# Two pairs' k and q loaded first, on two queues, and the steps of attention put in another order

## The chip, the cores and the metric

One core of a Trainium2 chip runs the kernel. Its engines work beside each other, each through its own queue in order: TensorE (PE) multiplies, VectorE (DVE) and ScalarE (ACT) work elementwise, GpSimd (POOL) as well, and SyncE (SP) issues most of the DMAs; ACT can issue DMAs too. The metric is the time of one execution in microseconds (us) on the device.

## What is computed

```python
# q, k, v: (4, 8, 576, 64), k drawn 8 times as large; M_prev, z_prev, beta: a memory per head
scores = np.where(causal, -1e9, scale * q @ k.T)
local = softmax(scores) @ v
q_p = phi(q)                                   # elu + 1
mem_out = (q_p @ M_prev) / (q_p . z_prev + 1e-6)
g = sigmoid(beta)
x = g * mem_out + (1 - g) * local              # then (2304, 512): tokens by heads and columns
x = mish(x @ moe_w_in) @ moe_w_out             # 512 -> 2048 -> 512
return silu(x @ moe2_w_in) @ moe2_w_out
```

## The kernel before

**Attention** goes by pairs of heads: 4 batches of 4 pairs, 16 pairs. For each pair four loads bring the transposed k (`ldkT`, 128 x 640, 320 KB), the transposed q (`ldqT`, 288 KB), q by rows (`ldnq`, 288 KB) and v (`ldnv`, 320 KB). With the `nq` of a batch's first pair come z (256 KB, one row spread over all partitions) and y (two loads of 64 KB in pieces of 64 numbers). The host lays the inputs out for this.

Per pair, TensorE makes the scores in five blocks of queries (`s40` and `s41` for two halves of the widest, `s3`, `s2`, `s1`, and the small `s0`), each for both heads, into a ring `s` of four PSUM buffers (line 581, `s0` line 620). VectorE masks a block and takes its row minimum in one instruction (`r...`, line 574) into a ring `sm` of four buffers in SBUF; ScalarE takes the exponentials (`e...`, line 601). TensorE transposes the probabilities (`X1` to `X3`, `W`, `RT`, line 482), VectorE and ScalarE copy these out, and TensorE multiplies with v (`Vhi`, `Vlo`, line 678). Beside that runs the memory part: relu of q on ScalarE (`phu`, line 503), a subtraction on GpSimd (`phn`, line 501), an exponential on ScalarE (`phe`, line 502), then products with z and y on GpSimd and a sum on VectorE (`phr`, line 509).

**The gates.** Beta goes through an exponential on ScalarE (`gate exp`, line 430), five small steps on VectorE (`sig`, lines 433 to 437) and five copies on ScalarE (`spread`, lines 442 to 448). Pair 0's `phg`, `n00` and `zg` wait for them.

**The two layers** follow from about 180 us on (lines 950 to 1075). They use products of pairs of blocks, and need TensorE nearly all of the time. The weights of the first quarter of the first layer are decoded on VectorE during attention (lines 779 to 807).

**What sets the order.** `Steps.plan` simulates the engines, each with durations given by hand, and at each moment lets an engine take the ready step with the smallest key: the latest time at which it may start, plus a shift from the table `SHIFT` (by step and by pair, found by search). The result is the order in which each engine's instructions are issued. A load in the plan takes SP 1.4 to 1.6 us and lands 2.2 us later. Three loads are treated apart: pair 0's `ldkT` and `ldqT` are issued in `consts` ahead of the plan and count as landed at 4.7, pair 0's `ldnq` at 4.9, beta at 5.2.

At the start ACT's queue issues pair 0's k; SP's queue pair 0's q, then beta, and then what the plan says: pair 0's q by rows with z and y, pair 1's q and k, pair 1's q by rows, pair 0's v and so on.

Of the kernel before, what the change touches and what calls it, by code (L numbers as in the profile page):

```python
# [336 lines left out]
class Attn:  # L337
    GATED = ("phg", "n00", "zg")
    RINGS = {"s": 4, "t": 4, "sm": 4}
# [60 lines left out]
    def consts(self):  # L400
# [20 lines left out]
        self.load(0, "kT", nc.scalar)  # L421
        self.load(0, "qT")
# [67 lines left out]
    def steps(self, p):  # L490
# [6 lines left out]
        for nm in ("kT", "qT", "nq", "nv"):  # L497
            f["ld" + nm] = None if p == 0 and nm in ("kT", "qT") else lambda nm=nm: self.load(p, nm)
# [192 lines left out]
    def register(self, m):  # L691
# [3 lines left out]
        m.add(("gate", "exp"), "A", 0.2, [], exp, 25.0, 5.2)  # L695
        m.add(("gate", "sig"), "D", 1.0, [("gate", "exp")], sig, 26.0)
        m.add(("gate", "spread"), "A", 1.0, [("gate", "sig")], spread, 28.0)
        for p in range(B * NP):
            f = self.steps(p)
            due = (p + 2) * self.T  # L700
            for n, (e, d, deps, lag) in self.pair.ops.items():
                deps = [(p, x) for x in deps] + ([("gate", "spread")] if p == 0 and n in self.GATED else [])
                if p > 1 and n in ("s40", "s41"):
                    deps += [(p - 2, x) for x in self.SC + ["s0"]]
                if p == 0 and n in ("ldkT", "ldqT"):
                    d, lag = 0.0, 4.7
                if p == 0 and n == "ldnq":
                    d, lag = 0.6, 4.3
                m.mode[p, n] = 2 if n in self.VA else 3 if n == "s0" else 1 if e == "P" else 0
                m.add((p, n), e, d, deps, f[n], due, max(0.0, (p - 2) * self.T), lag, self.pair.cols.get(n))  # L710
            for r, h, fs, ls in self.pair.uses:
                m.hold("A." + r, (p, h), [(p, x) for x in fs], [(p, x) for x in ls])
            for r, (_, _, fs, ls, _) in self.TILES.items():
                m.hold("A." + r, p, [(p, x) for x in fs], [(p, x) for x in ls], order=p)
# [197 lines left out]
class Moe:  # L912
# [324 lines left out]
    ('gate', 'exp'): -539.87, ('gate', 'sig'): 1632.4, ('gate', 'spread'): 1083.76, ('a', 'ldkT'): -342.43,  # L1237
# [217 lines left out]
```

## Time and profile before

| | us |
|---|---|
| median of 3 runs | 953.03 (952.82 to 953.31) |
| the profiled execution | 955.01 |
| its span, first to last instruction | 953.2 |
| busy: TensorE | 926.1 (97%) |
| busy: VectorE | 670.5 (70%) |
| busy: ScalarE | 504.8 (53%) |
| busy: GpSimd | 143.2 (15%) |

The shares are means over stages. In the chain of work that ended last TensorE has 85%, VectorE 8%, ScalarE 4% and DMA 1%. The page cuts the span into 40 slices: VectorE and ScalarE are nearly full in the first seven, GpSimd too, and from the ninth on TensorE is full and the others are not. Rows of a timeline give the start, the duration, the engine and line, output and inputs, shapes, the count and in brackets how long the engine had stood idle and what ended that.

### The profile page before, as it was taken

The page shows a single profiled execution, that of the slowest core. Times are in us where ns is not written, and L with a number is a line of the kernel's source. Part 1 is how long each engine was busy: PE and PEld are TensorE (multiplying, and loading weights), DVE is VectorE, ACT ScalarE, POOL GpSimd, SP SyncE. Part 2 cuts the span into 40 slices and gives each one's busy share as a digit, 9 for nine tenths or more (in the row PEclk, how much of TensorE's full clock was granted, in tenths as well). Part 3 has the DMA queues.
Part 4 walks back from the last instruction along what each step waited for, and adds up shares of the span by engine and source line. Part 5 has one row for each costly group of instructions (what it writes and reads, how often), then busy time and mean ns, then how long its engine had stood idle before and what let it go on. Part 6 is the DMA issues. An engine that isn't in the chain of part 4 may idle for free.

```text
span 953.2 us, 17388 instructions
## 1 busy us (share of the span) xinstructions
PE 926.1 (97%) x6656; PEld 817.2 (86%) x6656; DVE 670.5 (70%) x1536; ACT 504.8 (53%) x1188; POOL 143.2 (15%) x175
## 2 busy tenths in 40 slices
PE   5989999899999999999999999999999999999998
PEld 3666666599999999999999999898999898989986
DVE  4899999897386759654957899866656765754333
ACT  5999999777455333434433647554434442433330
POOL 5778987400000000000000000000000000000000
PEclk9999999899999999999999999999999999999999
DMA  6545452456447612760375535704550374024412
GB/s 220 146 154 157 146 170 62 147 232 250 171 135 240 216 45 73 258 194 1 96 254 189 231 119 194 293 23 139 204 182 3 109 257 157 1 89 149 156 56 99
DMA packets 57219, 143.47 MB, mean 151 GB/s; under 512 B 6960, under 2 KB 24368, under 8 KB 57136
## 3 DMA queue, kind: packets, MB, share of 16 engines
q1 hardware_dynamic: 56992, 142.04, 43.7%
q8 instruction: 52, 0.85, 0.4%
q10 hardware_dynamic: 144, 0.33, 0.1%
q14 instruction: 31, 0.25, 0.1%
HBM read 104.60 MB, written 37.75 MB: 149 GB/s over the span
## 4 chain that ended last, share of the span: by engine, by line
PE 85%; DVE 8%; ACT 4%; issue 2%; DMA 1%; SPq 0%; POOL 0%; DVEq 0%; ACTq 0%; POOLq 0%
PE acc L1054 42%; PE psX L986 7%; PE psX L987 7%; PE psX L988 7%; PE psY L986 4%; PE psY L987 4%; PE psY L988 4%; DVE sm L574 2%; PE ps_t L678 2%; PE psW L987 2%; PE psW L988 2%; PE psW L986 2%; PE ps_s L581 2%; ACT Ph L601 1%; PE ps_t L482 1%
## 5 line engine op out<-in xcount | busy, mean ns | idle before, releaser
L1054 PE MATMUL acc<-g,w 128*128 128x320 f32 (+1 forms) x1152 | 218.9, 337 | 0.0
L1054 PE MATMUL acc<-w,g 128*128 128x512 f32 x864 | 214.4, 394 | 0.0
L1054 PEld LDWEIGHTS acc<-g,w 128*128 128x128 f32 x1152 | 183.9, 188 | 13.1
L1054 PEld LDWEIGHTS acc<-w,g 128*128 128x128 f32 x864 | 157.8, 188 | 30.5
L1017 ACT COPY vt<-psX 128x256 f32<-128x256 f32 (+1 forms) x192 | 75.2, 398 | 161.5 <-PE psX L988 154.9
L1075 DVE TENSOR_TENSOR xT<-acc,xT 128x512 f32<-128x512 f32 (+1 forms) x126 | 77.1, 613 | 93.0 <-PE acc L1054 92.2
L1027 DVE TENSOR_TENSOR g<-vt,g 128x512 fp32r<-128x512 f32 (+1 forms) x128 | 94.2, 754 | 34.7 <-ACT g L1026 33.8
L1015 DVE TENSOR_TENSOR vt<-psY,vt 128x256 f32<-128x256 f32 (+1 forms) x128 | 57.9, 456 | 85.4 <-ACT vt L1017 44.8
L1026 ACT CAST g<-vt 128x512 fp32r<-128x512 f32 (+1 forms) x128 | 83.3, 672 | 32.4 <-PE acc L1054 31.1
L987 PE MATMUL psX<-x,w 128*128 128x320 f32 (+1 forms) x256 | 76.3, 298 | 1.4 <-DVE x L950 1.4
L986 PE MATMUL psX<-x,w 128*128 128x320 f32 (+1 forms) x256 | 76.3, 298 | 0.0
L988 PE MATMUL psX<-x,w 128*128 128x320 f32 (+1 forms) x256 | 76.1, 297 | 0.0
L581 PE MATMUL ps_s<-kT,qT 64*128 64x288 f32 (+3 forms) x320 | 66.9, 474 | 7.2 <-DMA kT<-in_kT_dram 4.8
L1023 ACT ACTIVATE vt<-vt 128x512 f32<-128x512 f32 (+1 forms) x64 | 43.9, 685 | 49.0 <-DVE vt L1015 48.9
L574 DVE CUSTOM_DVE_ANT_0 sm<-ps_s,mask 128x192 f32<-128x192 f32 (+3 forms) x128 | 56.8, 470 | 7.0 <-PE ps_s L581 3.9
L1021 ACT ACTIVATE vt<-vt 128x256 f32<-128x256 f32 (+1 forms) x64 | 28.5, 445 | 62.0 <-DVE vt L1015 62.0
L1015 DVE TENSOR_TENSOR vt<-psW,vt 128x256 f32<-128x256 f32 (+1 forms) x64 | 29.1, 455 | 37.0 <-PE psW L988 36.6
L1022 ACT ACTIVATE vt<-psX 128x256 f32<-128x256 f32 (+1 forms) x64 | 26.0, 407 | 51.1 <-PE psX L988 50.9
L987 PEld LDWEIGHTS psX<-x,w 128*128 128x128 f32 x256 | 48.8, 191 | 3.3 <-DVE x L950 1.6
L986 PEld LDWEIGHTS psX<-x,w 128*128 128x128 f32 x256 | 48.6, 190 | 2.1 <-issue 0.3
L988 PEld LDWEIGHTS psX<-x,w 128*128 128x128 f32 x256 | 48.8, 191 | 0.0
L601 ACT ACTIVATE Ph<-sm,m 128x448 f32<-128x448 f32 (+1 forms) x64 | 46.2, 725 | 3.0 <-DVE m L574 2.8
(125 smaller groups left out, 2040.3 us busy)
## 6 DMA issues: line engine op xcount, KB each, us to landing
stg<-in_moe_w_in_dram SPq DMA_DIRECT2D x32, 512.0 KB, 4.9
stg<-in_moe_w_out_dram SPq DMA_DIRECT2D x32, 512.0 KB, 3.7
x<-sp SPq DMA_DIRECT2D x18, 640.0 KB, 4.3
x<-sp SPq DMA_DIRECT2D x18, 512.0 KB, 4.2
sp<-x SPq DMA_DIRECT2D x12, 640.0 KB, 4.0
sp<-x SPq DMA_DIRECT2D x12, 512.0 KB, 3.5
nv<-in_v_dram SPq DMA_DIRECT2D x16, 320.0 KB, 3.0
x1T<-sp01T SPq DMA_DIRECT2D x8, 640.0 KB, 5.3
```

What stands on the lines that cost most here:

```text
L574: nc.vector.tensor_tensor_reduce(out, ps, mask, -0.125, init, ALU.add, ALU.min, acc)
L581: nc.tensor.matmul(ps, lhsT=s["qT"][R[j], qcols(i)], rhs=s["kT"][R[j], k0 + cols.start:k0 + cols.stop], start=True, stop=True)
L601: nc.scalar.activation(ptile(i)[:, o:o + w] if i else G("P0")[:, 2], s[f"sm{i}{j}"], AF.Exp, bias=s[f"m{i}"][:, j:j + 1], scale=-1.0, accu ...
L986: nc.tensor.matmul(o, lhsT=W(0, kc), rhs=X(0, kc), start=(n in (1, 2, 7) and kc == 0), stop=False, skip_group_check=True)
L987: nc.tensor.matmul(o, lhsT=W(0, kc), rhs=X(1, kc), start=False, stop=False, skip_group_check=True)
L988: nc.tensor.matmul(o, lhsT=W(1, kc), rhs=X(0, kc), start=False, stop=(kc == 1), skip_group_check=True)
L1015: nc.vector.tensor_tensor(o, self.bank[q, to], o, op=ALU.add)
L1017: f[f"s{n}"] = lambda n=n: nc.scalar.copy(val(*at[n]), self.bank[q, "X"])
L1026: f[f"h{c}"] = lambda c=c: nc.scalar.copy(hi(c), val(c))
L1027: f[f"l{c}"] = lambda c=c: nc.vector.tensor_tensor(self.gt(q, c)[:, 1, :2 * tb], val(c), hi(c).bitcast(F32), op=ALU.subtract)
L1054: nc.tensor.matmul(y, lhsT=a, rhs=b, start=(c == 0 and k == 0), stop=(c == 1 and k == 5))
L1075: nc.vector.tensor_tensor(part, acc, part, op=ALU.add)
```

## The change

In `consts`, both pairs 0 and 1 have their transposed k loaded from ACT's queue and their transposed q from SP's; pair 0's q by rows with z and y comes next, and beta last. The planner is told when these land (`FIRST`), takes beta's exponential as possible from 8.5 on instead of 5.2, and issues no other load before 4.2. The table `SHIFT` has other values for the steps of attention, the splits of the first layer's first block and the first group of weights; for the rest of the two layers it is the same. (`SHIFT` is left out here but for its first lines.)

```diff
--- before.py
+++ after.py
@@ -336,6 +336,7 @@
 
 class Attn:
     GATED = ("phg", "n00", "zg")
+    FIRST = {(0, "ldkT"): 4.7, (0, "ldqT"): 4.7, (1, "ldkT"): 6.2, (1, "ldqT"): 6.2, (0, "ldnq"): 7.0}
     RINGS = {"s": 4, "t": 4, "sm": 4}
     SC = ["s40", "s41", "s3", "s2", "s1"]
     VA = ["Vhi", "Vlo"]
@@ -418,8 +419,10 @@
                 compare_op=ALU.is_ge, fill=-8.0e9, base=0, channel_multiplier=1)
         for nm, w in (("bt0", H), ("g", H), ("g1", H), ("g1c", H), ("g1s", NP), ("btg", H), ("bt9", NP * 9)):
             setattr(self, nm, cp.tile([P, w], F32, name=nm))
-        self.load(0, "kT", nc.scalar)
-        self.load(0, "qT")
+        for p in range(2):
+            self.load(p, "kT", nc.scalar)
+            self.load(p, "qT")
+        self.load(0, "nq")
         nc.sync.dma_start(self.bt0, self.beta.unsqueeze(0).to_broadcast([P, H]))
 
     def gates(self):
@@ -495,7 +498,7 @@
         f = {}
         G = lambda nm: self.get(p, nm)
         for nm in ("kT", "qT", "nq", "nv"):
-            f["ld" + nm] = None if p == 0 and nm in ("kT", "qT") else lambda nm=nm: self.load(p, nm)
+            f["ld" + nm] = None if (p, "ld" + nm) in self.FIRST else lambda nm=nm: self.load(p, nm)
         mid = slice(ST, S)
 
         f["phn"] = lambda: nc.gpsimd.tensor_tensor(self.get(p, "e"), s["nq"], s["u"], op=ALU.subtract)
@@ -692,7 +695,7 @@
         m.cap.update({"A." + r: c for r, c in self.RINGS.items()})
         m.cap.update({"A." + r: t[4] for r, t in self.TILES.items()})
         exp, sig, spread = self.gates()
-        m.add(("gate", "exp"), "A", 0.2, [], exp, 25.0, 5.2)
+        m.add(("gate", "exp"), "A", 0.2, [], exp, 25.0, 8.5)
         m.add(("gate", "sig"), "D", 1.0, [("gate", "exp")], sig, 26.0)
         m.add(("gate", "spread"), "A", 1.0, [("gate", "sig")], spread, 28.0)
         for p in range(B * NP):
@@ -702,12 +705,10 @@
                 deps = [(p, x) for x in deps] + ([("gate", "spread")] if p == 0 and n in self.GATED else [])
                 if p > 1 and n in ("s40", "s41"):
                     deps += [(p - 2, x) for x in self.SC + ["s0"]]
-                if p == 0 and n in ("ldkT", "ldqT"):
-                    d, lag = 0.0, 4.7
-                if p == 0 and n == "ldnq":
-                    d, lag = 0.6, 4.3
+                if (p, n) in self.FIRST:
+                    d, lag = 0.0, self.FIRST[p, n]
                 m.mode[p, n] = 2 if n in self.VA else 3 if n == "s0" else 1 if e == "P" else 0
-                m.add((p, n), e, d, deps, f[n], due, max(0.0, (p - 2) * self.T), lag, self.pair.cols.get(n))
+                m.add((p, n), e, d, deps, f[n], due, max(4.2 if n[:2] == "ld" and (p, n) not in self.FIRST else 0.0, (p - 2) * self.T), lag, self.pair.cols.get(n))
             for r, h, fs, ls in self.pair.uses:
                 m.hold("A." + r, (p, h), [(p, x) for x in fs], [(p, x) for x in ls])
             for r, (_, _, fs, ls, _) in self.TILES.items():
@@ -1234,105 +1235,106 @@
 PERIOD = 10.582
 SHIFT = {
-    ('gate', 'exp'): -539.87, ('gate', 'sig'): 1632.4, ('gate', 'spread'): 1083.76, ('a', 'ldkT'): -342.43,
...
+    ('gate', 'exp'): 1735.81, ('gate', 'sig'): 1394.41, ('gate', 'spread'): 2479.26, ('a', 'ldkT'): 598.09,
+    ('ap', 0): -1603.22, ('a', 'ldqT'): -382.33, ('a', 'ldnq'): -652.91, ('a', 'ldnv'): 1784.43,
...
```

## Rows read from the trace of the kernel before

**Rows 1.** Busy time by stage: us, each engine's busy us (instructions), granted clock, DMA.

```profile
core 0: us, PE busy (x) PEld busy (x) DVE busy (x) ACT busy (x) POOL busy (x), PEclk, DMA share, GB/s
...
12.35:20.00 7.65, 6.55 (x44) 4.67 (x44) 4.71 (x27) 7.57 (x24) 6.73 (x7) 1.00 0.51 163
20.00:180.00 160.00, 148.89 (x1863) 102.17 (x1862) 153.38 (x541) 151.70 (x460) 130.95 (x156) 1.00 0.45 137
180.00:190.00 10.00, 8.65 (x61) 5.74 (x57) 7.83 (x15) 5.34 (x11) 0.36 (x1) 0.66 0.64 256
...
260.00:953.00 693.00, 688.73 (x4225) 636.16 (x4224) 453.00 (x865) 292.79 (x596) 0.00 (x0) 1.00 0.42 143
```

**Rows 2.** Timeline of TensorE, first 15 us: pair 0's scores, both `s0`, `s41`.

```profile
4.79 2.83 PE L581 MATMUL ps_s<-kT,qT 64*128 64x288 f32 x8 [4.79 <-DMA kT<-in_kT_dram]
11.66 0.69 PE L620 MATMUL ps_s<-kT,qT 64*64 64x64 f32 x8 [4.04 <-DMA kT<-in_kT_dram]
12.79 1.47 PE L581 MATMUL ps_s<-kT,qT 64*128 64x288 f32 x4 [0.43 <-DVE m L574]
```

**Rows 3.** Timeline: DMA issues of ACT's and SP's queues in the first 6 us.

```profile
0.90 0.38 ACTq L457 DMA_DIRECT2D kT<-in_kT_dram  x1
...
1.18 0.42 SPq L423 DMA_DIRECT2D bt<-in_beta_dram  x1
1.64 0.43 SPq L457 DMA_DIRECT2D nq<-in_q_dram  x1
...
2.59 1.39 SPq L466 DMA_DIRECT2D y<-in_z_prev_dram  x2
...
4.67 0.43 SPq L457 DMA_DIRECT2D kT<-in_kT_dram  x1
5.24 0.33 SPq L457 DMA_DIRECT2D nq<-in_q_dram  x1
```

**Rows 4.** DMA issues, us to landing: pair 0's k, q rows, y; pair 1's k; batch 1's y.

```profile
kT<-in_kT_dram ACTq DMA_DIRECT2D x1, 320.0 KB, 3.8
...
nq<-in_q_dram SPq DMA_DIRECT2D x1, 288.0 KB, 4.7
...
y<-in_z_prev_dram SPq DMA_DIRECT2D x1, 64.0 KB, 7.3
...
kT<-in_kT_dram SPq DMA_DIRECT2D x1, 320.0 KB, 6.9
...
y<-in_z_prev_dram SPq DMA_DIRECT2D x2, 64.0 KB, 3.6
```

**Rows 5.** Timeline of VectorE: the first gate step, two reductions of scores.

```profile
7.15 0.17 DVE L433 TENSOR_SCALAR bt<-bt 128x8 f32<-128x8 f32 x1 [6.29 <-ACT bt L430]
...
8.98 0.62 DVE L574 CUSTOM_DVE_ANT_0 sm<-ps_s,mask 128x448 f32<-128x448 f32 x1
...
14.40 0.46 DVE L574 CUSTOM_DVE_ANT_0 sm<-ps_s,mask 128x288 f32<-128x288 f32 x1 [1.52 <-PE ps_s L581]
```

**Rows 6.** Timeline of ScalarE: relus of pairs 0 and 1, first and last gate copy.

```profile
6.34 0.68 ACT L503 ACTIVATE u<-nq 128x576 f32<-128x576 f32 x1 [4.11 <-DMA nq<-in_q_dram]
...
9.05 0.22 ACT L442 COPY bt<-btg 128x32 f32<-128x32 f32 x1 [1.93 <-DVE btg L437]
...
9.57 0.18 ACT L448 COPY g1s<-g 64x4 f32<-64x4 f32 x1
...
12.35 0.68 ACT L503 ACTIVATE u<-nq 128x576 f32<-128x576 f32 x1 [2.60 <-DMA nq<-in_q_dram]
```

**Rows 7.** DMA from 0 to 20 us in slices of 0.5 us: GB/s.

```profile
GB/s 0 0 0 51 134 198 387 389 158 287 343 236 103 100 111 214 341 363 361 343 400 391 388 390 398 360 298 141 52 23 0 124 276 189 0 0 51 143 384 340
```

**Rows 8.** Timeline of TensorE, later: four score matmuls of 288 columns.

```profile
26.66 0.73 PE L581 MATMUL ps_s<-kT,qT 64*128 64x288 f32 x4
```

196 rows, old and new, of the table SHIFT are left out of this document.

## The prediction

> **What bounds the kernel now.** I read the page first (shares of engines, the slices, the chain that ended last), then the busy times by stage, then the timeline of the first 20 us engine by engine, then the DMA issues, their times to landing and the bytes per half microsecond. The stages differ. From 260 us to the end TensorE is busy 688.73 of 693 us [rows 1]: whatever the first part saves or loses is passed on to the end one for one. From 20 to 180 us, the attention, VectorE is busy 153.38 and ScalarE 151.70 of 160 us, TensorE 148.89 at gaps of their making [rows 1]: two engines share the bound, each with 6.6 to 8.3 us to spare in all. So work that these two can do before 20 us is what can be gained, and only there.
>
> Before 20 us they do little. TensorE makes pair 0's first scores from 4.79 to 7.62 and then stands 4.04 us until pair 1's k has landed [rows 2], because that load is issued at 4.67, behind beta, q, z and y on SP's queue [rows 3], and takes 6.9 us where pair 0's took 3.8 [rows 4]. VectorE's first reduction of scores starts at 8.98, behind the beta chain (7.15 to 8.98) in its queue [rows 5]. ScalarE relus pair 0's q at 6.34 and then waits in order for pair 1's q until 12.35; the exponentials come behind that [rows 6]. From 12.35 to 20 ScalarE is full (7.57 of 7.65), VectorE idle for 7.65 - 4.71 = 2.9 us [rows 1].
>
> **The change, part by part.**
> Pair 1's k and q move ahead of pair 0's q rows, z, y and beta. k and q of a pair are 320 + 288 KB = 0.62 MB. While ACT's and SP's first loads run together the engines move 387 to 389 GB/s; over 3.0 to 6.0 us the six slices average 300 [rows 7]. Pair 0's k lands at 0.90 + 3.8 = 4.7 as now. The next 0.62 MB take 1.6 us at 389 or 2.1 at 300: pair 1 lands at 6.3 to 6.8, I take 6.4. TensorE is busy with pair 0 until 7.62, so its 4.04 us of waiting are gone; what is late next are the four PSUM buffers of scores, that is VectorE's reductions.
>
> Pair 0's q rows have that 0.62 MB ahead of them: they landed at 1.64 + 4.7 = 6.34 [rows 4, 6]; now two loads of 0.3 MB later than pair 1's k would have them at 7.1 to 7.8. That is a loss of up to 1 us for relu and GpSimd's chain, hidden where ScalarE idles today (6.34 to 12.35).
>
> Pair 1's q rows, issued at 5.24 and landed at 12.35 now [rows 3, 6], are the point that decides. The loads ahead of them are the same nine in another order, so bytes give nothing. What can be won is the slack of the DMA engines: at 6.0 to 7.5 us they move 100 to 111 GB/s [rows 7], when y's small pieces are all that is queued; filled at 389 that is 1.5 us x 284 = 0.43 MB, 1.1 us. If all of 4.0 to 8.0 were filled (mean 194) it is 0.78 MB, 2.0 us. If y's pieces hold the queue all the same, nothing. So they land at 10.3 to 12.35, I take 11.25.
>
> ScalarE: it is full from the moment that load lands, so it gains 1.1 us (0 to 2.0). The first exponential of pair 0 no longer needs to stand behind it: +0.6. The planner believes that load to land at 4.2 + 1.6 + 2.2 = 8.0, so the relu can stand early in ScalarE's order; if it stands later, up to four more exponentials of 0.6 fit in front of it (+2.5). Against it, exp of beta and the five copies (9.05 to 9.75) [rows 6] lie in idle time today and in full time then: -0.9. Sum 0.8, up to 3.3 with the four; I take 2.0.
>
> VectorE: the first reduction follows the scores at 7.7 instead of 8.98, 1.3 us; the 2.9 us idle after 12.35 go, since pair 0's and pair 1's scores are there: 4.2. The beta chain (1.8 us) moves from the front into busy time: 2.4. If half of the idle time stays as waits for ScalarE, 0.9.
>
> Beta itself is last, behind y, which lands at 2.59 + 7.3 = 9.9 [rows 3, 4]; beta at 10 to 11 then. Behind the waiting exp on ScalarE stand exponentials, behind VectorE's five steps stand reductions. The exp can't hold ScalarE longer than pair 1's q rows do (11.25), so I cost the wait at nothing; without that cover it would be the about 1.5 us by which beta is later than the 8.5 that the planner is told.
>
> The order of attention's steps is new throughout, and the trace can't show it. I take 0 for pairs 2 to 15; the bounds are half of VectorE's idle time from 20 to 180, 6.6 / 2 = 3.3 us, either way. At the end of attention TensorE's granted clock is 0.66 for 10 us [rows 1], part of the time at 1.2 GHz; I leave it as it is. The loads of the later pairs and the weights change only their place in SP's order, where landing in a quiet stretch (y 3.6 us [rows 4]) has room.
>
> **Sum.** ScalarE 2.0 and VectorE 2.4, coupled by four buffers of scores: 2.2 us earlier from 20 us on. The profiled execution is 955.01 us (span 953.2 and 1.8 around it), so 952.8 for it; the median of the runs lies 1.98 below the profiled one, 953.03, so 953.03 - 2.2 = **950.8 us**. A measurement of this kernel can tell about 0.2% (1.9 us) from no change, which is nearly the whole of it.
>
> **Rivals.**
> A, the forecast: start-up shorter by 0.8 to 3.6 us, 949.4 to 952.2. For it: the three waits above and the two full engines after them.
> B, the start-up gives more: TensorE's early matmuls run at half the later rate. Four score matmuls of 288 columns take 1.47 us at 12.79 and 0.73 at 26.66 [rows 2, 8], though the row of the granted clock says 1.00 in both stretches [rows 1]; by the durations the first are at 1.2 GHz. TensorE is busy 6.55 us from 12.35 to 20 [rows 1]; with continuous work from 4.79 the rise may come before these, and give back half, 3.3 us, of which VectorE's wait for scores at 14.40 shows 1.5 on the path [rows 5]. With 2.5: 953.03 - 2.2 - 2.5 = 948.3, range 946.8 to 949.4. Against it: four PSUM buffers, so that a faster TensorE waits for VectorE. The Trainium skill (TensorE: Matmul & The Clock Gate, Part 1: The HAM clock gate) says that the slow state is the default and that activity releases it; the 1.47 against 0.73 agrees, and by that rule B would come about.
> C, the change doesn't do what it says for the bounding engines: pair 1's q rows land at 12.35 as now, since z, y and beta are still ahead of them, and ScalarE wins 0.6 and loses 0.9. Then 953.3; with a better or worse order 952.2 to 954.2. For it: the loads before it are the same.
> D, slower: the new order costs VectorE waits in the steady part. Place: pairs 2 to 15, 20 to 180 us. Price: VectorE idles 6.6 us there now; twice as much gives 953.03 - 2.2 + 6.6 = 957.4. It turns the sign from 2.2 / 14 = 0.16 us per pair on, and shows as slower from 0.3 us per pair. For it: both engines are so full that any wait counts. Against it: nothing in the loads of pairs 2 to 15 gets later.
>
> **How the numbers follow.** A 0.45, B 0.25, C 0.18, D 0.12. Faster by over 0.2% is below 951.1: all of B and 1.7 of A's 2.8 us, 0.25 + 0.29 = 0.54. Within 0.2%: the rest of A and C, 0.16 + 0.18 = 0.34. Slower: D, 0.12. The range reaches from B's lower end to C's upper, 946.8 to 954.2, and leaves out D; A's own range stands above.
>
> **What would show it.** In the profile after: TensorE with no wait of 4 us for k, and pair 1's k in SBUF by about 6.4; the first reduction on VectorE before 8; ScalarE's relu of pair 1 at about 11.25 and an exponential before it; VectorE busy about 2 us more before 20 us than its 7.6; the same 153 and 152 us of work in the attention and its end some 2 us earlier; TensorE's part after it as long as now. The forecast is wrong if ScalarE's relu still waits until past 12 us, if VectorE's idle time from 20 to 180 differs by over 2 us from 6.6, or if the stretch of low clock at 180 to 190 goes or grows: at 0.66 for 10 us it is worth up to 3.4 us.

## The result, and the profile after

| | before | after |
|---|---|---|
| median of 3 runs, us | 953.03 (952.82 to 953.31) | 960.26 (960.06 to 960.72) |
| profiled execution, us | 955.01 | 960.06 |
| its span, us | 953.2 | 958.3 |

After takes 1.0077 times as long as before (95% interval 1.0058 to 1.0095), 7.2 us more; 950.8 was forecast, with 946.8 to 954.2 as the range. The two profiled executions lie only 5.1 us apart, so the traces can account for 5.1: executions of one kernel differ with the granted clock (before took 951.1 to 952.4 us at a mean of 0.999 and 956.2 to 956.8 at 0.993 in later runs), and that of before was a long one, at 0.996.

Busy time by stage, after (columns as in [rows 1]):

```profile
core 0: us, PE busy (x) PEld busy (x) DVE busy (x) ACT busy (x) POOL busy (x), PEclk, DMA share, GB/s
...
20.00:70.00 50.00, 45.83 (x574) 31.70 (x573) 46.33 (x172) 48.26 (x145) 37.93 (x46) 1.00 0.45 134
70.00:90.00 20.00, 16.45 (x182) 10.47 (x184) 18.61 (x52) 15.72 (x45) 15.30 (x17) 0.91 0.49 153
90.00:110.00 20.00, 17.01 (x216) 11.47 (x214) 18.85 (x70) 17.60 (x57) 14.47 (x20) 1.00 0.33 100
110.00:180.00 70.00, 64.39 (x837) 45.24 (x833) 66.90 (x241) 67.56 (x207) 60.53 (x74) 1.00 0.40 130
180.00:190.00 10.00, 8.99 (x103) 6.74 (x101) 10.00 (x19) 5.34 (x13) 2.09 (x2) 1.00 0.51 160
260.00:958.00 698.00, 693.80 (x4258) 641.12 (x4256) 452.35 (x864) 294.89 (x600) 0.00 (x0) 1.00 0.41 142
```

The same stretches of the attention before, which [rows 1] gives only in sum:

```profile
core 0: us, PE busy (x) PEld busy (x) DVE busy (x) ACT busy (x) POOL busy (x), PEclk, DMA share, GB/s
20.00:70.00 50.00, 46.41 (x577) 31.57 (x574) 46.58 (x178) 46.94 (x144) 35.95 (x45) 1.00 0.54 162
70.00:90.00 20.00, 19.64 (x241) 12.92 (x236) 18.60 (x69) 19.65 (x62) 19.80 (x23) 1.00 0.58 176
90.00:110.00 20.00, 17.78 (x218) 12.22 (x220) 19.85 (x69) 18.54 (x54) 16.61 (x20) 1.00 0.34 109
110.00:180.00 70.00, 65.06 (x838) 45.46 (x836) 68.34 (x228) 66.58 (x203) 58.59 (x71) 1.00 0.38 116
```

One stretch stands out, 70 to 90 us. TensorE loses 19.64 - 16.45 = 3.2 us there, ScalarE 3.9, GpSimd 4.5. VectorE is busy as long as before, 18.61 against 18.60, but for 52 instructions and not 69: it did less in the same time. From 260 us on TensorE is as full as before, so what was lost ahead of that arrives at the end.

**The start.** Timelines of after, engine named in each line:

```profile
4.64 2.82 PE L584 MATMUL ps_s<-kT,qT 64*128 64x288 f32 x8 [4.64 <-DMA kT<-in_kT_dram]
8.31 1.02 PE L623 MATMUL ps_s<-kT,qT 64*64 64x64 f32 x8 [0.84 <-DVE m L577]
9.26 1.74 PE L584 MATMUL ps_s<-kT,qT 64*128 64x288 f32 x4
...
16.63 0.48 PE L623 MATMUL ps_s<-kT,qT 64*64 64x64 f32 x4 [2.28 <-DVE m L577]
...
6.96 0.68 ACT L506 ACTIVATE u<-nq 128x576 f32<-128x576 f32 x1 [4.72 <-DMA nq<-in_q_dram]
...
11.12 0.68 ACT L506 ACTIVATE u<-nq 128x576 f32<-128x576 f32 x1 [1.08 <-DMA nq<-in_q_dram]
...
16.34 0.22 ACT L445 COPY bt<-btg 128x32 f32<-128x32 f32 x1 [2.20 <-DVE btg L440]
...
7.62 0.62 DVE L577 CUSTOM_DVE_ANT_0 sm<-ps_s,mask 128x448 f32<-128x448 f32 x1 [6.76 <-PE ps_s L584]
...
12.83 0.48 DVE L436 TENSOR_SCALAR bt<-bt 128x8 f32<-128x8 f32 x1
...
13.59 1.09 DVE L438 TENSOR_SCALAR g<-g 128x8 f32<-128x8 f32 x1
14.71 1.32 DVE L439 TENSOR_SCALAR g1c<-g 128x8 f32<-128x8 f32 x1
...
13.24 2.76 POOL L507 TENSOR_TENSOR e<-e,u 128x576 f32<-128x576 f32 x2
...
31.69 0.42 DVE L685 TENSOR_TENSOR xT<-ps_t,R 128x256 f32<-128x256 f32 x1
```

The loads did what was forecast: pair 1's first scores, one of the two `s0` from 8.31 on, wait 0.84 us for a reduction and no longer for a DMA, where TensorE stood 4.04 us before [rows 2]; the relu of pair 1 runs at 11.12 instead of 12.35 [rows 6]. But the five gate steps took from 12.83 to 16.30. Where nothing disturbs them they take 0.17 to 0.20 us each (a run below has all five so). Here two that write 8 numbers per partition took 1.09 and 1.32 us, while GpSimd's two additions ran from 13.24 to 16.00, and the second ended with these. ScalarE's copies stood 2.20 us for them, TensorE's scores 2.28 us. The first product that VectorE writes into `xT` starts at 31.69, and in the trace of before at 31.74: nothing of the gain came through.

**The pile-up.** Timelines of after, 75 to 84 us:

```profile
76.48 2.03 DVE L801 TENSOR_SCALAR val<-val 128x512 f32<-128x512 f32 x1
78.43 0.48 DVE L577 CUSTOM_DVE_ANT_0 sm<-ps_s,mask 128x320 f32<-128x320 f32 x1
...
78.84 1.22 DVE L803 TENSOR_SCALAR val<-val 128x512 uint32<-128x512 uint32 x1
79.99 0.41 DVE L685 TENSOR_TENSOR xT<-ps_t,R 128x256 f32<-128x256 f32 x1
80.32 1.55 DVE L805 SCALAR_TENSOR_TENSOR val<-stg,val 128x512 uint32<-128x512 uint32 x1
...
76.02 1.06 POOL L633 TENSOR_TENSOR rx<-r,g1c 128x512 f32<-128x512 f32 x1
77.02 0.63 POOL L530 TENSOR_TENSOR Ph<-e,c 128x256 f32<-128x256 f32 x1
77.59 0.64 POOL L530 TENSOR_TENSOR Pl<-e,c 128x256 f32<-128x256 f32 x1
...
80.45 0.46 PE L485 MATMUL ps_t<-ident,rx 64*128 64x64 f32 x7 [1.89 <-DVE xT L685]
...
82.62 0.48 PE L485 MATMUL ps_t<-ident,Pl 64*128 64x64 f32 x4 [1.17 <-DVE W L478]
...
80.95 0.65 ACT L475 COPY R<-ps_t 128x256 f32<-128x256 f32 x2 [1.34 <-PE ps_t L485]
```

Three steps of the weights' decoding (`b0`, `b1`, `b2` of the job (0,2,0)) take 2.03 + 1.22 + 1.55 = 4.80 us. The first, from 76.48 to 78.51, ends 0.3 us behind the last of GpSimd's three instructions beside it (76.02 to 78.23). The product for `xT` stands behind the second step, and TensorE waits 1.89 us for it; a copy stands behind the third, and TensorE waits 1.17. ScalarE waits for TensorE's results in turn. Before, the same three steps ran later, farther apart, and two of them at full speed:

```profile
82.03 0.41 DVE L800 TENSOR_SCALAR val<-val 128x512 f32<-128x512 f32 x1
84.23 0.42 DVE L802 TENSOR_SCALAR val<-val 128x512 uint32<-128x512 uint32 x1
86.34 1.49 DVE L804 SCALAR_TENSOR_TENSOR val<-stg,val 128x512 uint32<-128x512 uint32 x1
```

GpSimd was not idler then (19.80 of 20 us); the steps met it at other instants.

### The profile page after: what moved, and what is told of

Its sections match the earlier page's. It is cut to its first block, busy times and chain, and to the rows that moved or that the text cites. A ratio compares the mean times of both kernels' runs of the same rounds, so it can differ in the third digit from the quotient of the medians.

```text
span 958.3 us, 17399 instructions
## 1 busy us (share of the span) xinstructions
PE 926.4 (97%) x6656; PEld 817.5 (85%) x6656; DVE 673.8 (70%) x1536; ACT 504.9 (53%) x1188; POOL 143.0 (15%) x175
## 4 chain that ended last, share of the span: by engine, by line
PE 83%; DVE 9%; ACT 4%; issue 2%; POOL 1%; DMA 0%; DVEq 0%; POOLq 0%; ACTq 0%
PE acc L1055 41%; PE psX L987 7%; PE psX L988 7%; PE psX L989 7%; PE psY L988 3%; PE psY L987 3%; PE psY L989 3%; PE ps_s L584 2%; DVE sm L577 2%; PE ps_t L681 2%; PE psW L988 2%; PE psW L989 2%; PE psW L987 2%; PE ps_t L485 2%; ACT Ph L604 1%
## 5 line engine op out<-in xcount | busy, mean ns | idle before, releaser
L577 DVE CUSTOM_DVE_ANT_0 sm<-ps_s,mask 128x448 f32<-128x448 f32 (+3 forms) x128 | 57.3, 472 | 13.2 <-PE ps_s L584 10.3
L584 PEld LDWEIGHTS ps_s<-kT,qT 64*128 64x128 f32 x320 | 34.2, 201 | 16.2 <-DVE m L577 7.2
```

Of the source, the lines that this page charges most:

```text
L577: nc.vector.tensor_tensor_reduce(out, ps, mask, -0.125, init, ALU.add, ALU.min, acc)
L584: nc.tensor.matmul(ps, lhsT=s["qT"][R[j], qcols(i)], rhs=s["kT"][R[j], k0 + cols.start:k0 + cols.stop], start=True, stop=True)
```

## The experiments

Each kernel was timed against the kernel before on the same chip; the ratio to before is what is compared (after: 1.0077). Beside it stands the lag: VectorE writes 32 products into `xT` (line 685 of after), and the lag is the start of the n-th of them, in order of time, less its start before. It comes from one execution each. The last two columns give durations of VectorE's steps: of the step on `z` (9 columns) that starts between 69 and 76 us, and the sum of the three decode steps of the job (0,2,0).

| kernel | ratio (95%) | lag at the 8th (67.0 us) | 9th (72.7) | 12th (86.0) | 15th (104.3) | 27th (166.5) | 32nd (190.1) | `z`, us | decode, us |
|---|---|---|---|---|---|---|---|---|---|
| after | 1.0077 (1.0058 to 1.0095) | 0.2 | 2.0 | 6.3 | 7.1 | 6.6 | 6.5 | 0.68 | 4.80 |
| old_order_new_loads | 1.0007 (0.9991 to 1.0024) | 2.4 | 2.4 | 3.5 | 2.2 | 2.3 | -0.2 | 0.70 | 1.67 |
| new_order_old_loads | 1.0071 (1.0047 to 1.0095) | 0.0 | 3.5 | 5.4 | 6.3 | 5.7 | 5.6 | 3.13 | 1.79 |
| new_until70_then_old | 1.0014 (1.0000 to 1.0028) | 0.2 | 3.7 | 6.0 | 4.8 | 3.6 | 2.3 | 3.12 | 1.74 |
| old_until70_then_new | 1.0099 (1.0079 to 1.0119) | 1.0 | 1.0 | 8.0 | 8.8 | 8.2 | 8.2 | 0.71 | 3.84 |
| new_70_to_110 | 1.0081 (1.0059 to 1.0102) | 0.7 | 0.7 | 7.7 | 8.5 | 8.5 | 7.7 | 0.70 | 3.83 |
| new_order_gates_moved | 1.0062 (1.0043 to 1.0081) | -1.9 | 1.6 | 3.5 | 4.4 | 3.8 | 3.8 | 3.14 | 1.80 |
| decode_left_out | 1.0043 (1.0026 to 1.0059) | 0.2 | 2.0 | 2.2 | 3.0 | 3.2 | 3.1 | 0.68 | none |
| other_decode_left_out | 1.0050 (1.0033 to 1.0067) | -0.6 | 1.2 | 5.6 | 6.4 | 5.8 | 5.6 | 0.68 | 4.81 |
| decode_later | 1.0057 (1.0035 to 1.0080) | 0.2 | 3.7 | 3.3 | 6.7 | 7.0 | 6.8 | 3.14 | 1.82 |
| gpsimd_four_left_out | 1.0026 (1.0016 to 1.0036) | 0.5 | 1.7 | 2.8 | 3.6 | 3.9 | 3.7 | 0.99 | 2.51 |
| old_order_decode_early | 1.0019 (1.0008 to 1.0030) | 2.3 | 2.3 | 4.9 | 3.2 | 3.3 | 0.8 | 0.70 | 2.93 |

The last lag sets every kernel against a stretch of half clock that before's execution has at 180 to 190 us [rows 1]; `old_order_gates_moved`, below, shows it to be worth some 2.5 us.

**Loads or order?** `old_order_new_loads` has the loads of after, and the planner settings and the `SHIFT` of before:

```diff
-                if (p, n) in self.FIRST:
-                    d, lag = 0.0, self.FIRST[p, n]
+                if p == 0 and n in ("ldkT", "ldqT"):
+                    d, lag = 0.0, 4.7
+                if p == 0 and n == "ldnq":
+                    d, lag = 0.6, 4.3
...
-        m.add(("gate", "exp"), "A", 0.2, [], exp, 25.0, 8.5)
+        m.add(("gate", "exp"), "A", 0.2, [], exp, 25.0, 5.2)
...
```

> The order of every engine's steps is that of the kernel before; only the loads are those of the changed kernel (pair 1's k and q, then pair 0's q rows with z and y, beta last). If the new order of attention's steps costs the 7 us (theory O), this one is near the kernel before: 950.5 to 954.5, a little faster where ScalarE starts pair 1's relu at about 11 instead of 12.35, a little slower where beta's exponential, second in ScalarE's queue, now waits for beta until about 11. If the loads cost it (theory L: beta last, or the shared DMA engines), 957 to 961.

`old_order_beta_early` is the same with beta issued ahead of pair 0's q rows:

```diff
+        nc.sync.dma_start(self.bt0, self.beta.unsqueeze(0).to_broadcast([P, H]))
         self.load(0, "nq")
-        nc.sync.dma_start(self.bt0, self.beta.unsqueeze(0).to_broadcast([P, H]))
```

> As the run before it, but beta is issued behind pair 1's q and ahead of pair 0's q rows. Theory O: 949 to 953, up to 2 us below the run with beta last, since beta's exponential stands second in ScalarE's queue. Theory L with beta as its cause: 950 to 953 here and 957 or more with beta last. Theory L with the shared DMA engines: 957 to 961 in both.

`new_order_old_loads` has the order of after and the loads of before:

```diff
-        for p in range(2):
-            self.load(p, "kT", nc.scalar)
-            self.load(p, "qT")
-        self.load(0, "nq")
+        self.load(0, "kT", nc.scalar)
+        self.load(0, "qT")
```

> The order of every engine's steps is that of the changed kernel; the loads are issued as in the kernel before (pair 1's q and k behind beta, pair 0's q rows, z and y). Theory O: 959 to 965, the changed kernel's time or some us more, since pair 1's k lands at 11.6 again. Theory L: 952 to 955.

`new_loads_old_shift` is after with the table of before:

```diff
 SHIFT = {
-    ('gate', 'exp'): 1735.81, ('gate', 'sig'): 1394.41, ('gate', 'spread'): 2479.26, ('a', 'ldkT'): 598.09,
+    ('gate', 'exp'): -539.87, ('gate', 'sig'): 1632.4, ('gate', 'spread'): 1083.76, ('a', 'ldkT'): -342.43,
...
```

> The changed kernel with the table of shifts of the kernel before: the planner is told of the new landing times, the order follows from that and was not sought. Theory O in its sharp form (any change of a landing time throws the whole order about, and the search got back only part): 960 to 970, slower than the changed kernel. If the old shifts keep most of the old order, 951 to 955. Theory L: 957 to 961.

Measured: 954.53, 954.55, 960.22 and 967.73 us (ratios 1.0007 with 0.9991 to 1.0024, 1.0007 with 0.9989 to 1.0026, 1.0071, and 1.0142 with 1.0112 to 1.0173). So the loads alone are worth nothing that could be told, and the order costs some 7 us, whatever the loads. The last run says how brittle the order is: the same table with four other landing times gives another order that is worse by another 6 us.

**Which part of the order?** In the next three the plan is made twice, by the settings of before and by those of after. Steps are taken from one order up to a planned time, then those still missing from the other; all have the loads of after.

```diff
-    m.issue()
+    want = spliced(m, old, CUTS)
+    order, late = feasible(m, want)
...
+CUTS = [("new", 70.0), ("old", None)]                  # new_until70_then_old
+CUTS = [("old", 70.0), ("new", None)]                  # old_until70_then_new
+CUTS = [("old", 70.0), ("new", 110.0), ("old", None)]  # new_70_to_110
```

> The loads of the changed kernel. The steps that its plan starts before 70 us in its own order, all that are left in the order of the kernel before. In the traces the two kernels are level at 60 us, and the changed one is 5 to 7 us behind from 95 us on. If the loss is made in the stretch from 72 to 95 us (theory M), this gives 953.5 to 956.5. If it was laid before 70 us and only shows later (theory S), or is spread over all pairs, 957 to 960.

> The counterpart: the loads of the changed kernel, the order of the kernel before up to 70 us of its plan, then the new order. Theory M: 958.5 to 961.5. Theory S: 954 to 956.5. Spread over all pairs: about 957.5.

> The loads of after; the steps planned from 70 to 110 us stand in the new order, all before and behind them in the order of before. If the loss is made in that stretch and stays, 958 to 962 us. If what stands behind 110 us in the new order is what keeps it from being made up again, the old order behind 110 us gives most of it back: 953 to 956.

Measured: 954.86, 962.80 and 962.64 us. What is new ahead of 70 us costs 1.3 us at most (ratio 1.0014, not told apart from the 1.0007 of the loads alone), what is new from 70 to 110 us alone costs as much as the whole, and what follows in the old order doesn't make it up. In the table it is the same place each time: between the 9th and the 12th product, 72.7 to 86.0 us before, the lag grows by 4.3 us in after and by 7.0 in the other two that have the new order only from 70 us on. (Stretches of half clock behind it are part of that; the last section has their price.) New until 70 us grows there too, by 2.3, but behind it the old order takes 2.4 us back by the 27th product.

Two other kernels with the new order throughout lose it a little earlier, and to another step. In `new_order_old_loads` (VectorE, GpSimd, TensorE):

```profile
71.45 3.13 DVE L628 TENSOR_SCALAR z<-z 128x9 f32<-128x9 f32 x1
...
78.03 0.63 DVE L799 TENSOR_SCALAR val<-val 128x512 f32<-128x512 f32 x1
...
79.00 0.42 DVE L801 TENSOR_SCALAR val<-val 128x512 uint32<-128x512 uint32 x1
...
81.18 0.74 DVE L803 SCALAR_TENSOR_TENSOR val<-stg,val 128x512 uint32<-128x512 uint32 x1
...
71.34 0.76 POOL L851 TENSOR_TENSOR val<-val 128x256 f32<-128x256 f32 x1
72.03 1.30 POOL L506 TENSOR_TENSOR u<-e,z 128x512 f32<-128x512 f32 x1
73.26 1.29 POOL L851 TENSOR_TENSOR w<-val,w 128x512 fp32r<-128x512 f32 x1
...
75.00 0.80 PE L582 MATMUL ps_s<-kT,qT 64*128 64x320 f32 x2 [1.42 <-DVE m L575]
```

The decode steps take 1.79 us and not 4.80. But the step on `z` lasts until GpSimd's three are through, 3.13 us, where in after it took 0.68, beginning at 71.59; reductions stand behind it, and TensorE waits 1.42 us. From the 8th to the 12th product the lag grows by 5.4 us, against 6.1 in after, and the ratio is 1.0071. `new_order_gates_moved` is the same (3.14 and 1.80 us, 5.4 us of lag, 1.0062). So the three decode steps are what was caught in after's execution, and the loss doesn't need them: the new order puts several of VectorE's steps beside a busy GpSimd, and not the same one is held each time. (`decode_later`, below, has after's loads and order up to there, and 3.14 us for `z` too; the traces don't show why after had 0.68.)

**Are the gate steps worth what the trace shows?** `new_order_gates_moved` has beta early, and the gates' steps moved forward in after's order, to where GpSimd is idle; `old_order_gates_moved` does the same in the order of before, with pair 1's relu behind pair 0's first exponential.

```diff
+MOVED = [
+    (('gate', 'exp'), [(0, 'e00')]),
+    (('gate', 'sig'), [('gate', 'exp'), (1, 'r00')]),
+    (('gate', 'spread'), [('gate', 'sig'), (1, 'e00')]),
+]
+    for k, anchors in MOVED:
+        want.remove(k)
+        want.insert(max(want.index(a) for a in anchors) + 1, k)
```

> The changed kernel with beta issued ahead of pair 0's q rows, and with the gates' steps moved in the order: the exponential and the five small steps of VectorE ahead of the reductions of the widest block, where VectorE now stands idle 1.5 us and GpSimd rests, and the copies behind pair 1's first exponential. If the gates' 3.2 us on VectorE (12.8 to 16.1, of which 2.2 beyond their own length) are what used up the gain of the early loads, the first product with v moves from 31.7 to 28.5 to 30 and the time falls by 1.5 to 3 us, to 957 to 959. If TensorE at its lower clock or ScalarE's full queue sets that point anyway, 31 to 32 and 960.

> The same on the order of the kernel before, with the loads of the changed kernel and beta early: the gates' steps of VectorE behind the small blocks' reductions, pair 1's relu behind pair 0's first exponentials. By the theory of the gates 950.5 to 953, 1.5 to 3 us below the run with beta early alone (954.5), and faster than the kernel before. If something else sets the start, 954 to 955.

Measured: 959.26 us (1.0062, 1.0043 to 1.0081) and 953.38 us (1.0001, 0.9986 to 1.0015), both just above what the theory of the gates gave. In the first the five steps take 0.17 to 0.20 us each, VectorE:

```profile
10.81 0.17 DVE L441 TENSOR_SCALAR g<-g 128x8 f32<-128x8 f32 x1
...
29.62 0.42 DVE L688 TENSOR_TENSOR xT<-ps_t,R 128x256 f32<-128x256 f32 x1
```

The first product starts 2.1 us earlier, as the forecast had it for the start (2.2). The total gains about 1 us, within the intervals' width; by the 9th product the step on `z` (3.14 us) has used the lead up.

**Is it the stretched steps, in after's execution?** `decode_left_out` leaves the three stretched decode steps out, `other_decode_left_out` the same three of another job, which ran at 0.41, 0.41 and 0.68 us.

```diff
+        if job == (0, 2, 0):        # other_decode_left_out: (0, 1, 0)
+            bits = dict(bits, b0=None, b1=None, b2=None)
```

> After, with three of VectorE's steps left out (the first three of the four that decode the job (0,2,0) of the weights, which took 2.03, 1.22 and 1.55 us between 76 and 82 us; at their shortest these take 0.41, 0.42 and 0.69). If their being stretched beside GpSimd makes the loss, the pile-up at 76 to 84 us goes and with it 4.8 us or more: 954 to 956. If the new order loses for other reasons, only their own 1.5 us can be won: 958.5 to 960.

> After, with the same three steps left out of the job (0,1,0), which ran at their shortest (0.41, 0.41 and 0.68 us between 51 and 56 us). It is the measure for what 1.5 us less of VectorE's work is worth by itself. By the theory of the stretched steps 958.5 to 960; if any relief of VectorE ahead of 76 us dissolves the pile-up, 954 to 956, as the one with the other job.

Measured: 957.69 and 959.43 us. The intervals overlap, so the times alone don't part them; the lags do. Without the stretched steps the pile-up is gone (from the 9th to the 12th product +0.2 us instead of +4.3), without the others it stays (+4.4). The forecast of 954 to 956 was missed by 2 us: some 3 us of lag are there without the pile-up. And 1.5 us less of VectorE's work elsewhere gives 1.0050 for 1.0077 with the pile-up in place (the intervals overlap), so not all of the gain need be the pile-up's.

`gpsimd_four_left_out` leaves VectorE as it is and takes four steps off GpSimd:

```diff
+        if (ph, pr) == (0, 0):
+            f["S2"] = f["S4"] = None
+            for x, a in (("S0", 3), ("S1", 5)):
+                f["l" + x] = lambda a=a: nc.sync.dma_start(
+                    out=span(1, a, 2).bitcast(F32), in_=span(0, a, 2).bitcast(F32))
```

> After, with four of GpSimd's steps taken off it: of the steps that combine the first pair of weights, the two sums that ran 0.75 and 0.76 us at 71.5 and 75.3 us are left out, and the two differences that ran 1.29 and 1.26 us at 73.4 and 78.5 us are a copy by a DMA. VectorE's steps all stand as in after. If the neighbour on GpSimd is what stretches the three decode steps (2.03, 1.22, 1.55 us at 76 to 82 us), they fall to under 2.5 us together and the kernel to 956 to 958.5; if they keep 4 us or more together without these neighbours, the stretching has another cause, and 959.5 to 961.

Measured: 956.79 us. VectorE and its neighbour:

```profile
76.16 0.52 DVE L801 TENSOR_SCALAR val<-val 128x512 f32<-128x512 f32 x1
...
77.01 0.42 DVE L803 TENSOR_SCALAR val<-val 128x512 uint32<-128x512 uint32 x1
...
77.69 1.57 DVE L805 SCALAR_TENSOR_TENSOR val<-stg,val 128x512 uint32<-128x512 uint32 x1
...
77.23 1.49 POOL L504 TENSOR_TENSOR e<-nq,u 128x576 f32<-128x576 f32 x1
```

The same three instructions take 2.51 us instead of 4.80, and the one that still has a neighbour for its whole length is still long. The lag grows by 1.1 us in place of 4.3. The ratio falls from 1.0077 to 1.0026, two thirds of the loss; by the lag at the 15th product (3.6 for 7.1) it is half. The kernel also has 4.1 us less to do on GpSimd, and after's stretch of half clock at 82.5 is gone with the pile-up, so this is an upper bound for the stretching itself.

`decode_later` leaves nothing out and puts the four decode steps later and apart:

```diff
+MOVED = [
+    (('W', (0, 2, 0), 'b0'), [(7, 'r31')]),
+    (('W', (0, 2, 0), 'b1'), [(7, 'r30')]),
+    (('W', (0, 2, 0), 'b2'), [(6, 'phq')]),
+    (('W', (0, 2, 0), 'b3'), [(8, 'r410')]),
+]
```

> After, with the four decode steps of the job (0,2,0) about 8 us later in VectorE's order, spread out as in the order of before, and the two steps that need them behind them; nothing is left out. If the place of these steps makes the loss, 954 to 957. If the loss is made by the rest of the order between 70 and 100 us, 959 to 961. If the steps are stretched again at the new place, 959 to 962, and the trace shows it by their durations.

Measured: 959.99 us. Lines of ScalarE and VectorE:

```profile
93.55 0.62 ACT L870 CAST w<-val 128x512 fp32r<-128x512 f32 x1 [1.41 <-DVE val L816]
...
100.43 1.91 DVE L813 SCALAR_TENSOR_TENSOR val<-stg,val 128x512 uint32<-128x512 uint32 x1
```

At the 12th product the lag is 3.3 us instead of 6.3, although here the step on `z` was held (3.14 us), and at the 15th it is back at 6.7: ScalarE now waits 1.41 us for the moved steps, and the next job's third step is stretched to 1.91. What the place won was given back by new waits. This execution had a granted clock of 1.00 from 20 to 950 us (mean 0.999) and took 960.41 us, where before took 951.1 to 952.4 at that mean; so the loss doesn't need the low clock either.

**Is the place alone enough?** `old_order_decode_early` is `old_order_new_loads` with the three steps moved the other way:

```diff
+MOVED = [
+    (('W', (0, 2, 0), 'b0'), [(5, 'X3Bh')]),
+    (('W', (0, 2, 0), 'b1'), [(7, 'r400')]),
+    (('W', (0, 2, 0), 'b2'), [(7, 'r401')]),
+]
```

> The loads of after with the whole order of before (954.5 us by itself), and only three steps moved in it: the first three decode steps of the job (0,2,0) stand 3.5 to 7 us earlier in VectorE's order and near one another, as in the order of after. If their place alone makes the loss, 957.5 to 960. If it only does together with what else the new order has between 70 and 110 us, 953.5 to 956.

Measured: 955.61 us; by the ratios 1.1 us more than without the move (1.0019 against 1.0007, intervals that overlap). The steps took 1.23, 0.85 and 0.85 us, the lag grew by 2.6 us at the 12th product (1.1 without the move), and most of it was gone at the 15th. The place alone costs some 1 us at most; the rest needs what else is new there.

**The best parts together.** `new_until70_gates_moved` joins the gates' places to the new order until 70 us and the old behind it:

```diff
+CUTS = [("new", 70.0), ("old", None)]     # with the MOVED of new_order_gates_moved
```

> Loads of after with beta ahead of pair 0's q rows, the new order up to 70 us with the gate steps moved as before, the order of before behind 70 us: the two parts that did best by themselves. If the 2 us that the start wins there are kept behind 70 us, 951 to 953; if the order of before takes up leads as it takes up lags, 953.5 to 956.

Measured: 954.28 us (949.64 to 955.44), ratio 0.9996 (0.9980 to 1.0011): no faster than before that could be told, as the forecast had it for an order that takes up leads.

## Why the prediction was wrong

**The loads: right.** Pair 0's q rows were forecast for 7.1 to 7.8 and came at 6.96, a little ahead of that, pair 1's for 11.25 and came at 11.12; the first reduction was forecast for 7.7 and came at 7.62; three exponentials fitted ahead of pair 1's relu.

**The gates: mis-sized.** They were costed at 1.8 us on VectorE and 0.9 on ScalarE. They took 3.5 on VectorE and held up ScalarE for 2.2. The row that could have warned was there, in the trace of before:

```profile
7.59 1.01 DVE L435 TENSOR_SCALAR g<-g 128x8 f32<-128x8 f32 x1
```

The other four took 0.17 to 0.20, and the 1.8 was taken over as a length without asking what this one had met (GpSimd's subtraction, from 7.16 to 8.57). "VectorE busy about 2 us more before 20 us" came true (9.44 against 7.63), and partly for that reason: busy time of a stretched instruction is waiting.

**The sum of 2.2: did not arrive.** The first product is where it was. With the gates moved it is 2.1 us earlier, and even that gives about 1 us at the end in the new order and nothing that could be told in the old.

**The order at 0 with bounds of 3.3: the step that failed.** The order costs some 7 us, with the new loads or the old. The bound was taken from VectorE's idle time, 6.6 us from 20 to 180 [rows 1]. Idle time can't bound it, because most of the loss stands in VectorE's busy time: in after 4.80 us for three steps that need 1.5, in `new_order_old_loads` 3.13 for one that took 0.68 in after. (The idle time grew too, from 6.6 to 160 - 150.7 = 9.3 us, over the 2 us named as a sign that the forecast is wrong.) Rival D had the direction and a price of 957.4, at a chance of 0.12; its place, all pairs from 2 to 15, was too wide: most of it is made in 20 us, from the 8th to the 12th product. In the chances, 1.7 of A's 2.8 us is 0.27 and not 0.29, which changes nothing here.

**The clock.** The low stretch at 180 to 190 us [rows 1] went, as the text had allowed for, and another came at 82.5 to 85.9, behind the pile-up. B did not come about: four score matmuls of 288 columns took 1.74 us at 9.26, no faster than the 1.47 of before [rows 2], although TensorE had been busy from 4.64 with gaps below 1 us. The prediction took the rule of the Trainium skill cited there (TensorE: Matmul & The Clock Gate, Part 1: The HAM clock gate), that activity releases the slow state, to mean that more work early brings the rise earlier; here it did not.

**What stays open.** Without the pile-up some 2.5 to 4 us remain (1.0026 and 1.0043). The lags put 1 to 2 us of it between the 8th and the 9th product and 1 to 2 between the 9th and the 15th. A part may be plain work that the new order has moved there: from the 8th to the 15th product VectorE starts 93 instructions in after and in `gpsimd_four_left_out`, and 88 in before (accumulator reads not counted), an estimated 2.4 us more by the shortest times of their forms. No run separates the causes, and none has the new order with nothing held at this place.

## What to carry to other kernels

When a change gives a planner new inputs, the new order is the change: weigh it by the steps that it puts beside other engines' work, not by the idle time of the fullest engine. Compare instructions of one form: on VectorE here, what a long one had beyond the shortest was mostly a wait, which busy time hides. And before a loss is put down to the steps that one trace shows, look at the same steps in another run of the same order. Time the edit with the old order and the new order without the edit before either is credited.

## What the hardware showed that was not expected

Some of VectorE's instructions last longer beside GpSimd's: the decode step of 512 columns took 0.41 to 2.03 us, a step of 8 columns 0.17 to 1.32, the step on `z`, of 9 columns, up to 3.14. RECIPROCAL stayed at 0.20 beside the same neighbours, as did reductions of scores from PSUM (0.48 at 78.43) and the product into `xT` (0.36 to 0.43 throughout). The Trainium skill (SBUF — State Buffer, Who interferes with whom) says that these two engines share a pair of ports, that `tensor_scalar` in its two-port modes and instructions with two SBUF inputs contend for it, and that whoever issues first holds it for the whole instruction. The lines agree on which instructions are long. Two go beyond what it says: the 2.03 us ended behind three GpSimd instructions in a row (76.02 to 78.23), and the 3.13 us of `z` in `new_order_old_loads`, to 74.58, with three in a row (71.34 to 74.55), not with the one that was running. In after the same step on `z` ended with the first (71.59 to 72.27, GpSimd's to 72.24).

TensorE's clock fell to half behind a stretch with little work. After, the stretch and the fall behind it:

```profile
79.00:82.50 3.50, 1.00 (x11) 0.55 (x11) 3.50 (x6) 2.08 (x8) 3.06 (x3) 1.00 0.56 162
82.50:85.90 3.40, 3.28 (x40) 2.60 (x40) 2.43 (x10) 1.71 (x5) 0.00 (x0) 0.50 0.92 308
```

The same in `old_order_new_loads`:

```profile
57.00:59.90 2.90, 0.90 (x13) 0.53 (x11) 2.87 (x6) 1.98 (x7) 2.90 (x4) 0.99 0.75 227
59.90:63.20 3.30, 3.30 (x47) 3.02 (x45) 2.56 (x10) 1.62 (x4) 2.53 (x3) 0.50 0.88 281
```

There the lag is 0.9 us up to the 6th product and 2.4 from the 7th on: 3.3 us at 1.2 GHz cost 1.5. It doesn't always: in `old_order_decode_early` the clock is 0.50 from 26.6 to 30.0 us too, and the lag is 0.9 before and behind that. In `old_order_gates_moved` the low stretch that before has at 180 to 190 us [rows 1] was not there, and its last product came 2.8 us earlier than that of before, having been 0.3 ahead until then.
